# Reordering loads, transposes and attention steps in the first two blocks of a fused linear-attention and gated feed-forward kernel

## The chip, the cores and the metric

The kernel runs on one core of a Trainium2 chip. The metric is the device time of one execution in microseconds (us). The core's engines are TensorE (PE, with its weight loads as PEld), VectorE (DVE), ScalarE (ACT), GpSimd (POOL) and SyncE (SP); each takes its own instructions in the order in which the program lists them and waits on semaphores for the others. DMAs issued by POOL go to one software queue, those issued by SP to one hardware queue; both are served by the core's 16 DMA engines.

## What is computed

```
kv  = einsum('bhsd,bhse->bhde', k, v)        # 8 batches, 8 heads, 576 tokens, head size 64
out = einsum('bhsd,bhde->bhse', q, kv)
x   = out / sqrt(mean(out*out, -1) + 1e-6) * g_norm      # then tokens x 512
g, val = x @ w_gate, x @ w_val               # 512 -> 1536
ffn = (gelu(g) * val) @ w_out                # 1536 -> 512
y   = x + sigmoid(x @ w_res) * ffn           # 4608 tokens x 512, float32
```

Inputs and outputs are float32. The kernel computes in float16 with float32 accumulation; the loads by POOL convert on the way.

## The kernel before, in words

**Blocks.** Tokens come in nine blocks. Block b (0 to 7) holds the first 512 tokens of batch b, as `NJ` = 4 tiles of 128; block 8 holds the 64 tokens that are left over of each batch. Attention for a batch is computed one or two blocks ahead of the block's feed-forward part, and its steps are put between the feed-forward matmuls so that PE always has work. The order on every engine is written out by hand: nothing is scheduled afterwards.

**Steps of attention for batch b.** `load_batch` (L117) issues on POOL the DMAs of q (into `qraw`), k, v, the last 64 rows of k and v (`load_last_kv`, L107: tiles `kl`, `vl`, two sets used in turn) and, for batches from 4 on, two `qr` pieces of leftover q rows. `by_token` (L128) reorders q; `a_qT` on PE (batch 1) or `d_qT` (L376, a DMA transpose on SP) makes `qT`. `a_kv` (L219) multiplies k by v into `kv2`, 40 small matmuls and a copy. `a_o` (L224) multiplies `qT` by `kv2` into four PSUM tiles (`op`). `a_ss` (L263) squares them on ACT and sums on DVE; `a_norm` (L298) turns the sums into `1/rms` with Newton steps on DVE or POOL; `a_t` (L337) scales on DVE into `t`. `a_xT` (L350, PE and ACT, batch 1) or `d_xT` (L387, a DMA transpose on SP) makes `xT`; `a_g` (L366) multiplies by g afterwards on DVE.

**Feed-forward.** In block 0 up to f = 7 and in block 1, `m_gval` (L421) computes a 128-wide slice f of gate and value for all 512 tokens, `m_act` applies gelu on ACT and multiplies on DVE into `hid`. Later slices and blocks use `gv_group` (L920), a seven-product scheme for 2 x 2 quarters, whose sums of weights (`weight_sums`, `wo_sums`, `wr_sums`) are made on DVE in blocks 0 and 1. Its words such as "1g" or "h22" name products and evacuations; "h22" is the last of a group and runs on POOL (L986). Functions hung on a word run right behind it. The output product is `out_by_f` (L1004) in block 0: twelve steps f, each of four matmuls (one per token tile) into four PSUM banks; later blocks use `out_by_products` (L608), with PSUM tiles wA, wD, wE, wF.

**What sets the order around the change.** Each block has a list of slots, one per slice f or output step, and a dictionary `plan` from slot to functions that run behind it. `attn_plan_1` (L1324) puts batch 1's attention into block 0's output slots: slot `NF + 3` (NF = 12) is the last of the four res products, slot `NF + 4 + f` is output step f. `plan_attn_2` (L1369) puts batch 2's into block 1 (slot s = slice s), `plan_attn_ahead` (L1399) batch 3's into block 1 and the later ones two blocks ahead. The steps below the `for blk` loop (L1527) emit it all; behind slot 2 of block 0 it loads w_res, batch 1 and w_out.

**Queues.** POOL's DMAs use eight semaphores in turn, so an issue waits until the DMA eight before it has landed; what POOL has to do behind it waits too. `load_behind(b)` (L1354) first lets POOL copy one element of `qT` of batch b into a tile `hold`, which makes POOL wait for that transpose, and then issues the loads of batch b + 1. SP holds the DMA transposes and the stores of results, strictly in the order of the program.

Before, the order of POOL's loads in block 0 is w_res, q, k, v, kl, vl of batch 1, then w_out in pieces of 2, 2, 4 and 4 slices. SP's order in block 1 is: qT of batch 2, four stores, qT of batch 3, xT of block 2, xT of block 3. PE's order at the end of block 1 is: kv of batch 3, eight res products (`rps`), op of batch 3, eight res products, wA.

Of the kernel before, what the change touches and what calls it, by code (L numbers as in the profile page):

```python
# [14 lines left out]
RMS_EPS = 1e-6  # L15
# [3 lines left out]
def kernel(  # L19
# [94 lines left out]
        b16_t[b, "k"] = qkvp.tile(by_head, FP16, tag="k16", name="k16")  # L114
        b16_t[b, "v"] = qkvp.tile([P, H, NJ * D], FP16, tag="v16", name="v16")

    def load_batch(b):  # L117
        tiles_16(b)
        raw[b, "q"] = stage.tile([P, H, NJ * D], FP16, tag="qraw", name="qraw")
        nc.gpsimd.dma_start(out=raw[b, "q"], in_=rows4(q, b, 0, H))  # L120
        nc.gpsimd.dma_start(out=b16_t[b, "k"], in_=rows4(k, b, 0, H))
        nc.gpsimd.dma_start(out=b16_t[b, "v"], in_=rows4(v, b, 0, H))
        load_last_kv(b)
        if pair(b) is not None:
            load_qr(2 * pair(b))
            load_qr(2 * pair(b) + 1)

    def by_token(b, copy=nc.vector.tensor_copy, js=slice(0, NJ)):  # L128
        copy(
# [168 lines left out]
    def a_norm(b, j0, j1, eng=nc.vector):  # L298

        s = st[b]  # L300
        if "rinv" not in s:
            s["rinv"] = attnp.tile([P, NJ + 1, H], FP32, tag="ny", name="ny")
        ss, yy = (t[:, j0:j1, :].rearrange("p j h -> p (j h)") for t in (s["ss"], s["rinv"]))
        n = (j1 - j0) * H
        m = attnp.tile([P, (NJ + 1) * H], FP32, tag="nm", name="nm")[:, 0:n]
        a = attnp.tile([P, (NJ + 1) * H], FP32, tag="na", name="na")[:, 0:n]
        mh = attnp.tile([P, (NJ + 1) * H], FP32, tag="nh", name="nh")[:, 0:n]
        magic = 0x5F1FFFF9 if eng is nc.gpsimd else 0x5F3759DF
        eng.tensor_scalar(out=m, in0=ss, scalar1=1.0 / D, scalar2=RMS_EPS, op0=ALU.mult, op1=ALU.add)
# [3 lines left out]
        if eng is nc.gpsimd:  # L313
            for step in range(2):
                eng.tensor_tensor(out=a, in0=yy, in1=yy, op=ALU.mult)
                eng.tensor_tensor(out=a, in0=a, in1=m, op=ALU.mult)
                c = (-0.703952253, 0.703952253 * 2.38924456) if step == 0 else (0.375, -1.25)
                eng.tensor_scalar(out=mh, in0=a, scalar1=c[0], scalar2=c[1], op0=ALU.mult, op1=ALU.add)
# [3 lines left out]
                eng.tensor_tensor(out=yy, in0=mh, in1=yy, op=ALU.mult)  # L322
            return
        eng.tensor_scalar(out=mh, in0=m, scalar1=-0.5, scalar2=None, op0=ALU.mult)
        for _ in range(3):
            eng.tensor_tensor(out=a, in0=yy, in1=yy, op=ALU.mult)
            eng.tensor_tensor(out=a, in0=a, in1=mh, op=ALU.mult)
            eng.scalar_tensor_tensor(out=yy, in0=a, scalar=1.5, in1=yy, op0=ALU.add, op1=ALU.mult)

    def pair(b):  # L330

        return b - B // 2 if b >= B // 2 else None
# [14 lines left out]
            scale = rinv[:, NJ, :, None].to_broadcast([P, H, D])  # L347
        nc.vector.tensor_tensor(out=t, in0=o, in1=scale, op=ALU.mult)  # L348

    def a_xT(b, j):  # L350
# [5 lines left out]
        nc.scalar.activation(  # L356
            out=xT_t[blk][:, jj, :, :], in_=ps, func=AF.Copy, scale=gcol
        )

    def a_x(b, j, eng=nc.vector):  # L360
        row_times_g(*where(b, j), eng)
# [56 lines left out]
                stop=(cc == NP - 1 and j1 == NJ),  # L418
            )

    def m_gval(blk, f, pool=pmoe, tag="mm"):  # L421
        if f == 0:
            hids[blk] = hidp.tile([P, NF, NJ * P], FP16, tag="hid", name="hid")
        gps = pool.tile([P, NJ * P], FP32, tag=tag, name="gps")
        m_mm(gps, wg_c, f, blk, 0, NJ)
        vps = pool.tile([P, NJ * P], FP32, tag=tag, name="vps")
        m_mm(vps, wv_c, f, blk, 0, NJ)
        m_act(blk, f, gps, vps)

    def m_res(blk, j, bank):  # L430
# [489 lines left out]
    def gv_group(blk, g, banks, amid, order):  # L920
# [67 lines left out]
        for word in ORDERS[order].split():  # L988
# [12 lines left out]
            for f in amid.get(word, ()):  # L1001
                f()

    def out_by_f(blk):  # L1004

        ths, fpss, pfs, banks = [], [], [], {}

        def res(j):
            if j == 0:
                banks.update(banks_behind())  # L1010
            ths.append(m_res(blk, j, banks[j]))

        slots = [lambda j=j: res(j) for j in range(NJ)]

        def step(f):
            if f == 0:
                fpss.extend(pmoe.tile([P, C], FP32, name="fps", bank=banks[n]) for n in "ADEF")
                pmoe.turn = [banks[n] for n in "ADEF"]
            for j in range(NJ):
                m_ffn(blk, j, f, fpss[j])  # L1020
            if NFH <= f < NFH + NJ:
# [302 lines left out]
    def attn_plan_1():  # L1324

        b = 1
        ss = [lambda j=j: a_ss(b, j) for j in range(NJ)]
        t = [lambda j=j: a_t(b, j) for j in range(NJ)]
        x = [lambda j=j: a_xT(b, j) for j in range(NJ)]
        plan = {  # L1330
            NF - 1: [lambda: by_token(b)],
            NF + 3: [
                lambda: attn_begin(b),
                lambda: a_qT(b, 0),
                lambda: a_qT(b, 1),
                lambda: load_batch(b + 1),
                lambda: a_kv(b),
                *[lambda j=j: a_x(0, j) for j in range(NJ)],
            ],
            NF + 4: [lambda: a_o(b), ss[0], ss[1]],  # L1340
            NF + 5: [ss[2], ss[3]],
            NF + 6: [lambda: a_norm(b, 0, NJ), t[0], t[1], t[2], t[3]],
            2 * NF: [x[0], x[1]],
            2 * NF + 1: [x[2]],
            2 * NF + 2: [x[3], lambda: wo_sums(0), lambda: wo_sums(2)],
        }
        return plan

    plans = [{} for _ in range(B + 1)]
# [19 lines left out]
    def plan_attn_2():  # L1369
        b, m = 2, 1  # L1370
        act = nc.scalar.copy
        at(m - 1, 2 * NF + 3, lambda: by_token(b, act, slice(0, 2)))
        at(m, 0, lambda: by_token(b, act, slice(2, 4)), lambda: attn_begin(b), lambda: d_qT(b))
        at(m, 2, lambda: a_kv(b))
        at(m, 3, lambda: load_behind(b))
        at(m, 1, lambda: wo_sums(1))
        at(m, 3, lambda: wo_sums(3))
        at(m, 4, lambda: a_o(b))
        for j in range(NJ):
            at(m, 4 + j // 2, lambda j=j: a_ss(b, j))  # L1380
        at(m, 6, lambda: a_norm(b, 0, NJ, nc.gpsimd))
        for j in range(NJ):
            at(m, 9 + j // 2, lambda j=j: a_t(b, j))
        at(m, 10, lambda: d_xT(b, 0, NJ))
        for i in range(2):
            amid_out.setdefault(m, {}).setdefault("00", []).insert(i, lambda i=i: a_g(b, 2 * i, 2 * i + 2))

# [11 lines left out]
    def plan_attn_ahead(b):  # L1399
# [22 lines left out]
        else:  # L1422
            at(m, 8, lambda: by_token(b, act, slice(0, 2)))
            at(m, 9, lambda: by_token(b, act, slice(2, 4)), *begin)
            at(m, NF - 1, lambda: a_kv(b, act))
            at(m, NF, lambda: load_behind(b))
        if rem:
            at_word(m + 2, 0, "cv", lambda: a_g(b, NJ, NJ + 1))
            own = 2 * pair(b) + 1 == b
# [3 lines left out]
                at_word(m, last, "3g", lambda: rem_mm(b))  # L1433
            at_word(m, last, "g12", lambda: rem_out(b))
        else:
            at(m, NF, lambda: a_o(b), lambda: a_ss(b, 0), lambda: a_ss(b, 1))
            aside_out(m, "D", lambda: a_ss(b, 2), lambda: a_ss(b, 3))
        aside_out(m, "F", lambda: a_norm(b, 0, NJ + rem, pool))
        first = [lambda: new_block(b), lambda: a_t(b, 0), lambda: a_t(b, 1)]
# [23 lines left out]

    units = [(n, g) for g in (1, 2, 0) for n in "gv"]
    sums = {u: weight_sums(u, nc.vector) for u in units}
    for slot, u in ((2, ("g", 1)), (4, ("g", 2)), (NF - 1, ("v", 1))):
        for i in range(2):
            at(0, slot + i, *sums[u][2 * i : 2 * i + 2])
    at(0, 6, *sums["v", 2][0:2])
    at_word(0, 0, "1v", *sums["v", 2][2:4])  # L1470
    late_sums = [f for u in (("g", 0), ("v", 0)) for f in sums[u]]
    for i, f in enumerate(late_sums[0:6]):
        at(1, (2, 6, 7)[i // 2], f)
    aside_out(1, "D", *late_sums[6:8])
    for blk in GROUPS:
        t = token_sums(blk, nc.vector)
# [50 lines left out]
    for blk in range(B + 1):  # L1527
# [21 lines left out]
        else:  # L1549
# [25 lines left out]

                plan.setdefault(NF - 2, []).append(banks_ahead)
            if blk == 1:
                slots[0] = lambda: m_gval(1, 0, pattn, "at")
            outs = []
            slots += [lambda i=i: outs[i]() for i in range(4 if blk < B else 2)]  # L1580
            if not groups:
                plan.setdefault(NFH + 2, []).insert(0, lambda: s_begin(blk))

            def products(blk=blk, outs=outs):
                if not res_in_halves(blk) and not res_and_attn(blk):
# [18 lines left out]
        for s in range(len(slots)):  # L1604
# [42 lines left out]
```

## Time and profile before

| what | value |
|---|---|
| median of three runs | 321.18 us (320.92 to 321.63) |
| span of the profiled execution, first to last instruction | 319.6 us |
| difference to the median, taken as what lies around the span | 1.6 us |
| PE / DVE / ACT / POOL busy | 309.5 / 275.2 / 210.8 / 188.0 us |
| granted TensorE clock over the span | 0.999 |
| PE's idle time that a wait for vl ended, at 42 us | 0.28 us |
| PE's idle time that a wait for w_out ended, at 43 us | 0.63 us |
| block 0's output products, first and last | 43.53, 54.61 us |
| block 1's slices (`m_gval`), first to the end of the last | 55.55 to about 77.8 us |
| op of batch 3 / first output product of block 1 | 80.49 / 82.80 us |
| first product of block 2 | 91.97 us |

The profile lists instruction groups with engine, source line, output and input tiles. A bracket behind a row of the timeline gives how long the engine had been idle before it, and whose event ended that. Matmuls overlap in time: their pace is read from start to start (0.216 us for 512 columns, 0.109 for 256), not from the duration of one.

### The profile page before, as it was taken

To read this page: it belongs to the slowest core of one execution; us is meant where nothing else is said; L and a number is where in the kernel's file an instruction comes from. 1 tells how busy PE (TensorE), PEld (TensorE's weight loads), DVE (VectorE), ACT (ScalarE), POOL (GpSimd) and SP (SyncE) were. 2 spreads that over 40 slices of the span, in tenths; PEclk is the share of its full clock that TensorE was granted. 3 is DMA by queue.
4 is the path that set the end of the run, shared out by engine and by line. 5 is a ranking of instruction groups with operands and counts; after the bars stand their busy time and mean duration, and the time that the engine had idled before them with its cause. 6 is when DMAs were issued, how large, how long until landed. Compare 5 with 4: busy or idle time off the path is not lost.

```text
span 319.6 us, 7753 instructions
## 1 busy us (share of the span) xinstructions
PE 309.5 (97%) x3039; PEld 245.6 (77%) x3039; DVE 275.2 (86%) x488; ACT 210.8 (66%) x385; POOL 188.0 (59%) x248
## 2 busy tenths in 40 slices
PE   7899989999999999999999999999999999999993
PEld 2544755444788888888888888888888888888882
DVE  5886979799898999989998999899988777897774
ACT  4763675456848794879587858795767467736770
POOL 2873350573769479756875887517761375396332
PEclk9999999999999999999999999999999999999999
DMA  7999999799994699479947694800340003000204
GB/s 253 328 192 202 195 203 196 162 153 189 171 118 82 199 138 97 82 216 128 105 84 215 88 145 71 226 6 0 68 148 2 0 3 132 2 2 40 93 0 131
DMA packets 77253, 38.89 MB, mean 122 GB/s; under 512 B 42146, under 2 KB 74914, under 8 KB 77218
## 3 DMA queue, kind: packets, MB, share of 16 engines
q0 software_dynamic: 39280, 17.17, 42.7%
q1 hardware_dynamic: 37360, 20.71, 24.8%
q10 hardware_dynamic: 578, 0.52, 0.5%
q8 instruction: 23, 0.38, 0.5%
q14 instruction: 12, 0.10, 0.1%
HBM read 38.80 MB, written 9.44 MB: 151 GB/s over the span
## 4 chain that ended last, share of the span: by engine, by line
PE 84%; DMA 11%; SPq 1%; POOL 1%; DVE 1%; issue 0%; DVEq 0%
PE Ag L949 12%; PE Av L949 11%; PE wA L518 11%; PE Fv L949 6%; PE Fg L949 6%; DMA wg<-in_moe_w_gate_dram 5%; DMA wo<-in_moe_w_out_dram 5%; PE rA L569 4%; PE gps L413 3%; PE fps L450 3%; PE vps L413 3%; PE Ev L949 3%; PE Eg L949 3%; PE wD L518 3%; PE wF L518 3%; PE wE L518 3%
## 5 line engine op out<-in xcount | busy, mean ns | idle before, releaser
L986 POOL TENSOR_TENSOR hid<-ge,c 128x512 f16<-128x512 f16 x22 | 25.6, 1164 | 37.9 <-ACT ge L980 37.9
L518 PEld LDWEIGHTS <-hid_s 128*128 128x128 f16 x384 | 37.6, 98 | 4.4
L949 PEld LDWEIGHTS <-wsv 128*128 128x128 f16 x352 | 34.1, 98 | 5.2 <-issue 1.1
L949 PEld LDWEIGHTS <-wsg 128*128 128x128 f16 x352 | 34.4, 98 | 4.0
L364 POOL TENSOR_TENSOR t<-t,g 128x512 f16<-128x512 f16 x32 | 37.1, 1188 | 0.0
L705 POOL TENSOR_TENSOR osb<-osb,t 128x512 f32<-128x512 f32 x28 | 34.1, 1246 | 0.0
L959 ACT COPY Eg<-Ag 128x512 f32<-128x512 f32 x22 | 12.8, 584 | 27.9 <-PE Ag L949 27.9
L518 PEld LDWEIGHTS <-hid 128*128 128x128 f16 x288 | 28.2, 98 | 3.5
L949 PEld LDWEIGHTS <-wg 128*128 128x128 f16 x264 | 25.8, 98 | 3.2
L949 PEld LDWEIGHTS <-wv 128*128 128x128 f16 x264 | 25.8, 98 | 3.0
L949 PE MATMUL Av<-ts,wsv 128*128 128x256 f16 x176 | 26.4, 272 | 0.1
L949 PE MATMUL Ag<-ts,wsg 128*128 128x256 f16 x176 | 26.4, 273 | 0.0
L970 DVE TENSOR_TENSOR Fg<-Ag,d 128x512 f32<-128x512 f32 x22 | 15.3, 697 | 11.0 <-ACT d L963 8.1
L261 DVE TENSOR_REDUCE ss<-sq 128x8 f32<-128x512 f32 x32 | 20.5, 679 | 2.4 <-ACT sq L256 2.4
L401 ACT ACTIVATE ge<-gps 128x512 f16<-128x512 f32 x20 | 11.9, 598 | 15.6 <-PE gps L413 13.6
L518 PE MATMUL wA<-wo_ts,hid_s 128*128 128x256 f16 x168 | 20.6, 273 | 0.0
L980 ACT ACTIVATE ge<-Eg 128x512 f16<-128x512 f32 x22 | 13.2, 598 | 9.9 <-PE Eg L949 9.9
L980 ACT ACTIVATE ge<-c 128x512 f16<-128x512 f32 x22 | 13.8, 627 | 7.7 <-DVE c L970 7.7
L413 PE MATMUL vps<-xT,wv 128*128 128x512 f16 x72 | 18.5, 379 | 0.4 <-DMA wv<-in_moe_w_val_dram 0.3
L348 DVE TENSOR_TENSOR t<-op,ny 128x512 f16<-128x512 f32 x28 | 18.4, 684 | 0.5 <-POOL ny L322 0.4
L970 DVE TENSOR_TENSOR c<-Ag,d 128x512 f32<-128x512 f32 x22 | 15.2, 689 | 3.9 <-PE Ag L949 3.8
L413 PE MATMUL gps<-xT,wg 128*128 128x512 f16 x72 | 18.5, 379 | 0.0
(220 smaller groups left out, 851.0 us busy)
## 6 DMA issues: line engine op xcount, KB each, us to landing
out_dram<-osb SPq DMA_DIRECT2D x14, 512.0 KB, 3.4
qraw<-in_q_dram POOLq DMA_DIRECT2D x7, 512.0 KB, 6.5
k<-in_k_dram POOLq DMA_DIRECT2D x7, 512.0 KB, 8.4
v<-in_v_dram POOLq DMA_DIRECT2D x7, 512.0 KB, 10.4
wg<-in_moe_w_gate_dram POOLq DMA_DIRECT2D x2, 512.0 KB, 9.5
wo<-in_moe_w_out_dram POOLq DMA_DIRECT2D x2, 512.0 KB, 13.6
out_dram<-osb SPq DMA_DIRECT2D x4, 256.0 KB, 3.8
wv<-in_moe_w_val_dram POOLq DMA_DIRECT2D x3, 256.0 KB, 8.5
```

What stands on the lines that cost most here:

```text
L261: nc.vector.tensor_reduce(out=out_, in_=sqs.pop((b, i)), op=ALU.add, axis=mybir.AxisListType.X)
L348: nc.vector.tensor_tensor(out=t, in0=o, in1=scale, op=ALU.mult)
L364: eng.tensor_tensor(out=t_t[blk][:, jj, :], in0=t_t[blk][:, jj, :], in1=g16, op=ALU.mult)
L413: nc.tensor.matmul(ps[:, j0 * P : j1 * P], lhsT=w[:, cc, :], rhs=xT_t[blk][:, j0:j1, cc, :], start=(cc == 0 and j0 == 0), stop=(cc == NP - ...
L518: nc.tensor.matmul(ps[:, e - es[0], :], lhsT=a[:, f, e * P : (e + 1) * P], rhs=b[:, f, :], start=(start and e == es[0] and f == 0), stop=( ...
L569: nc.tensor.matmul(out_[:, e, :], lhsT=x_[:, e, cc, :], rhs=w_[:, cc, :], start=(first and e == 0 and cc == 0), stop=(cc == 1), skip_group ...
L705: nc.gpsimd.tensor_tensor(out=res_all[of], in0=res_all[of], in1=t_t[blk][of], op=ALU.add)
L949: nc.tensor.matmul(out_[:, r, :], lhsT=lhsT, rhs=rhs, start=(first and r == 0 and c == 0), stop=(c == 1), skip_group_check=True,)
L959: nc.scalar.copy(out=tile_of("E", u), in_=ps["A", u])
L970: nc.vector.tensor_tensor(out=dst, in0=ps["A", u], in1=sb["d", u], op=ALU.add)
L980: nc.scalar.activation(out=ge[q], in_=source(q, "g"), func=AF.Gelu)
L986: eng.tensor_tensor(out=dst, in0=ge[q], in1=source(q, "v"), op=ALU.mult)
```

## The change

- **Loads in block 0.** `load_batch` calls `amid()` between k and v; for batch 1 that loads w_out's first three slices. The rest of w_out follows in pieces of 1, 2, 3 and 3. For all batches the two `qr` pieces go ahead of k.
- **Batch 1's attention** goes amid the output products of block 0. `a_kv` runs behind output step 2 with its copy on ACT; `a_o` and the squares behind the second matmul of step 3; norm and `t` behind step 4; the four `a_xT` behind step 10, amid step 11 (two, the second with its copy on DVE) and at its end. `out_by_f` gets hooks between its matmuls for that (`amid_step`). Block 1's first slice is multiplied in two halves of tokens.
- **`a_norm` on DVE** has nine instructions instead of twelve: the two steps that POOL used, with constants folded.
- **`wo_sums`**: all four in block 1 (slots 1, 1, 3, 4); before, two of them stood in block 0 and two in slots 1 and 3. `s_begin` in blocks without groups goes from slot 8 to slot 10; two late weight sums go from slots 6, 7 to 9, 10.
- **Batch 2**: op behind slot 5 instead of 4, norm on DVE behind slot 7 instead of on POOL behind slot 6, `t` in slots 8 and 9 instead of 9 and 10, `d_xT` behind slot 9 instead of 10. By that xT of block 2 stands ahead of qT of batch 3 in SP's order.
- **Batch 3**: kv behind the first eight res products, op behind all sixteen.
- **Batch 4's loads** wait on POOL for qT of batch 3 and also for xT of block 2; its kl and vl leave `load_batch` and are issued in block 2, behind the POOL product of group 1 ("h22").

```diff
-    def load_batch(b):
+    def load_batch(b, amid=lambda: None):
         nc.gpsimd.dma_start(out=raw[b, "q"], in_=rows4(q, b, 0, H))
-        nc.gpsimd.dma_start(out=b16_t[b, "k"], in_=rows4(k, b, 0, H))
-        nc.gpsimd.dma_start(out=b16_t[b, "v"], in_=rows4(v, b, 0, H))
-        load_last_kv(b)
         if pair(b) is not None:
             load_qr(2 * pair(b))
             load_qr(2 * pair(b) + 1)
+        nc.gpsimd.dma_start(out=b16_t[b, "k"], in_=rows4(k, b, 0, H))
+        amid()
+        nc.gpsimd.dma_start(out=b16_t[b, "v"], in_=rows4(v, b, 0, H))
+        if pair(b) != 0:
+            load_last_kv(b)
...
-        eng.tensor_scalar(out=mh, in0=m, scalar1=-0.5, scalar2=None, op0=ALU.mult)
-        for _ in range(3):
-            eng.tensor_tensor(out=a, in0=yy, in1=yy, op=ALU.mult)
-            eng.tensor_tensor(out=a, in0=a, in1=mh, op=ALU.mult)
-            eng.scalar_tensor_tensor(out=yy, in0=a, scalar=1.5, in1=yy, op0=ALU.add, op1=ALU.mult)
+        eng.tensor_tensor(out=a, in0=yy, in1=yy, op=ALU.mult)
+        eng.tensor_tensor(out=a, in0=a, in1=m, op=ALU.mult)
+        eng.scalar_tensor_tensor(out=mh, in0=a, scalar=2.38924456, in1=yy, op0=ALU.subtract, op1=ALU.mult)
+        eng.tensor_tensor(out=a, in0=mh, in1=mh, op=ALU.mult)
+        eng.tensor_tensor(out=a, in0=a, in1=m, op=ALU.mult)
+        eng.scalar_tensor_tensor(
+            out=yy, in0=a, scalar=1.25 / (0.375 * c**2), in1=a, op0=ALU.subtract, op1=ALU.mult
+        )
+        eng.scalar_tensor_tensor(
+            out=yy, in0=yy, scalar=1.875 / (0.375 * c**4), in1=mh, op0=ALU.add, op1=ALU.mult
+        )
...
         gps = pool.tile([P, NJ * P], FP32, tag=tag, name="gps")
-        m_mm(gps, wg_c, f, blk, 0, NJ)
         vps = pool.tile([P, NJ * P], FP32, tag=tag, name="vps")
-        m_mm(vps, wv_c, f, blk, 0, NJ)
+        for j in range(0, NJ, step):
+            m_mm(gps, wg_c, f, blk, j, j + step)
+            m_mm(vps, wv_c, f, blk, j, j + step)
...
                 lambda: load_batch(b + 1),
-                lambda: a_kv(b),
                 *[lambda j=j: a_x(0, j) for j in range(NJ)],
             ],
-            NF + 4: [lambda: a_o(b), ss[0], ss[1]],
-            NF + 5: [ss[2], ss[3]],
-            NF + 6: [lambda: a_norm(b, 0, NJ), t[0], t[1], t[2], t[3]],
-            2 * NF: [x[0], x[1]],
-            2 * NF + 1: [x[2]],
-            2 * NF + 2: [x[3], lambda: wo_sums(0), lambda: wo_sums(2)],
+            NF + 6: [lambda: a_kv(b, nc.scalar.copy)],
+            NF + 8: [lambda: a_norm(b, 0, NJ), *t],
+            2 * NF + 2: [x[0]],
         }
+        amid_step[3, 1] = [lambda: a_o(b), *ss]
+        amid_step[NF - 1, 1] = [x[1], lambda: a_xT(b, 2, nc.vector)]
+        amid_step[NF - 1, 3] = [x[3]]
...
-        at(m, 1, lambda: wo_sums(1))
-        at(m, 3, lambda: wo_sums(3))
-        at(m, 4, lambda: a_o(b))
+        at(m, 1, lambda: wo_sums(0), lambda: wo_sums(1))
+        at(m, 3, lambda: wo_sums(2))
+        at(m, 4, lambda: wo_sums(3))
+        at(m, 5, lambda: a_o(b))
         for j in range(NJ):
-            at(m, 4 + j // 2, lambda j=j: a_ss(b, j))
-        at(m, 6, lambda: a_norm(b, 0, NJ, nc.gpsimd))
+            at(m, 5 + j // 2, lambda j=j: a_ss(b, j))
+        at(m, 7, lambda: a_norm(b, 0, NJ))
         for j in range(NJ):
-            at(m, 9 + j // 2, lambda j=j: a_t(b, j))
-        at(m, 10, lambda: d_xT(b, 0, NJ))
+            at(m, 8 + j // 2, lambda j=j: a_t(b, j))
+        at(m, 9, lambda: d_xT(b, 0, NJ))
...
-            at(m, NF - 1, lambda: a_kv(b, act))
-            at(m, NF, lambda: load_behind(b))
+            at(m, NF, lambda: a_kv(b, act), lambda: load_behind(b, b - 1))
+            at_word(m + 1, 1, "h22", lambda: load_last_kv(b + 1))
...
-            at(m, NF, lambda: a_o(b), lambda: a_ss(b, 0), lambda: a_ss(b, 1))
+            at(m, NF + 1, lambda: a_o(b), lambda: a_ss(b, 0), lambda: a_ss(b, 1))
...
-        at(1, (2, 6, 7)[i // 2], f)
+        at(1, (2, 9, 10)[i // 2], f)
...
-                load_batch(1)
-                for f0, f1 in ((0, 2), (2, 4), (4, 8), (8, NF)):
+                load_batch(1, lambda: load_wo(0, 3))
+                for f0, f1 in ((3, 4), (4, 6), (6, 9), (9, NF)):
                     load_wo(f0, f1)
```

More of the change, by code (lines that the diff above doesn't have):

```diff
@@ L307, in a_norm @@
         mh = attnp.tile([P, (NJ + 1) * H], FP32, tag="nh", name="nh")[:, 0:n]
-        magic = 0x5F1FFFF9 if eng is nc.gpsimd else 0x5F3759DF
-        eng.tensor_scalar(out=m, in0=ss, scalar1=1.0 / D, scalar2=RMS_EPS, op0=ALU.mult, op1=ALU.add)
+        pool = eng is nc.gpsimd
+        c = 0.703952253
+        scaled = 1.0 if pool else (0.375 * c**5) ** -2
+        magic = 0x5F1FFFF9 if pool else 0x5F1FFFF9 - 2**31
+        eng.tensor_scalar(
+            out=m, in0=ss, scalar1=scaled / D, scalar2=scaled * RMS_EPS, op0=ALU.mult, op1=ALU.add
+        )
         eng.tensor_scalar(
@@ L312, in a_norm @@
         )
-        if eng is nc.gpsimd:
+        if pool:
             for step in range(2):
@@ L316, in a_norm @@
                 eng.tensor_tensor(out=a, in0=a, in1=m, op=ALU.mult)
-                c = (-0.703952253, 0.703952253 * 2.38924456) if step == 0 else (0.375, -1.25)
-                eng.tensor_scalar(out=mh, in0=a, scalar1=c[0], scalar2=c[1], op0=ALU.mult, op1=ALU.add)
+                of_a = (-c, c * 2.38924456) if step == 0 else (0.375, -1.25)
+                eng.tensor_scalar(out=mh, in0=a, scalar1=of_a[0], scalar2=of_a[1], op0=ALU.mult, op1=ALU.add)
                 if step == 1:
@@ L323, in a_norm @@
             return
-        eng.tensor_scalar(out=mh, in0=m, scalar1=-0.5, scalar2=None, op0=ALU.mult)
-        for _ in range(3):
-            eng.tensor_tensor(out=a, in0=yy, in1=yy, op=ALU.mult)
-            eng.tensor_tensor(out=a, in0=a, in1=mh, op=ALU.mult)
-            eng.scalar_tensor_tensor(out=yy, in0=a, scalar=1.5, in1=yy, op0=ALU.add, op1=ALU.mult)
+        eng.tensor_tensor(out=a, in0=yy, in1=yy, op=ALU.mult)
[8 more added lines that the diff above has]
+            out=yy, in0=yy, scalar=1.875 / (0.375 * c**4), in1=mh, op0=ALU.add, op1=ALU.mult
+        )
     def pair(b):
@@ L348, in a_t, with a_xT @@
         nc.vector.tensor_tensor(out=t, in0=o, in1=scale, op=ALU.mult)
-    def a_xT(b, j):
+    def a_xT(b, j, eng=nc.scalar):
         blk, jj = where(b, j)
@@ L355, in a_xT @@
             nc.tensor.transpose(ps[:, cc, :], t_t[blk][:, jj, cc * P : (cc + 1) * P], ident)
-        nc.scalar.activation(
-            out=xT_t[blk][:, jj, :, :], in_=ps, func=AF.Copy, scale=gcol
-        )
+        if eng is nc.scalar:
+            nc.scalar.activation(out=xT_t[blk][:, jj, :, :], in_=ps, func=AF.Copy, scale=gcol)
+        else:
+            eng.tensor_scalar(out=xT_t[blk][:, jj, :, :], in0=ps, scalar1=gcol, scalar2=None, op0=ALU.mult)
     def a_x(b, j, eng=nc.vector):
@@ L419, in m_mm, with m_gval @@
             )
-    def m_gval(blk, f, pool=pmoe, tag="mm"):
+    def m_gval(blk, f, pool=pmoe, tag="mm", step=NJ):
         if f == 0:
@@ L1002, in gv_group @@
                 f()
+    amid_step = {}
     def out_by_f(blk):
@@ L1020, in step @@
                 m_ffn(blk, j, f, fpss[j])
+                for g in amid_step.get((f, j), ()):
+                    g()
             if NFH <= f < NFH + NJ:
@@ L1465 @@
     sums = {u: weight_sums(u, nc.vector) for u in units}
-    for slot, u in ((2, ("g", 1)), (4, ("g", 2)), (NF - 1, ("v", 1))):
+    for slot, u in ((2, ("g", 1)), (5, ("g", 2)), (NF - 1, ("v", 1))):
         for i in range(2):
             at(0, slot + i, *sums[u][2 * i : 2 * i + 2])
-    at(0, 6, *sums["v", 2][0:2])
+    at(0, 7, *sums["v", 2][0:2])
     at_word(0, 0, "1v", *sums["v", 2][2:4])
@@ L1577 @@
             if blk == 1:
-                slots[0] = lambda: m_gval(1, 0, pattn, "at")
+                slots[0] = lambda: m_gval(1, 0, pattn, "at", NJ // 2)
             outs = []
@@ L1581 @@
             if not groups:
-                plan.setdefault(NFH + 2, []).insert(0, lambda: s_begin(blk))
+                plan.setdefault(NF - 2, []).insert(0, lambda: s_begin(blk))
             def products(blk=blk, outs=outs):
```

## The prediction

> **What bounds the kernel now.** First the page: busy shares, then the chain that ended last.
>
> ```profile
> PE 309.5 (97%) x3039; PEld 245.6 (77%) x3039; DVE 275.2 (86%) x488; ACT 210.8 (66%) x385; POOL 188.0 (59%) x248
> ...
> PE 84%; DMA 11%; SPq 1%; POOL 1%; DVE 1%; issue 0%; DVEq 0%
> ```
>
> PE (TensorE) is the bound: whatever makes PE wait lengthens the kernel one for one, and only an idle stretch of PE can be won. Work elsewhere costs nothing unless PE waits for it. So I read PE's timeline from 37 us on (earlier the two kernels are alike) for gaps.
>
> ```profile
> 41.62 0.32 PE L211 MATMUL kvp<-v,k 128*64 128x64 f16 x8
> 42.21 0.22 PE L211 MATMUL kvp<-vl,kl 128*64 128x64 f16 x2 [0.28 <-DMA vl<-in_v_dram]
> ...
> 43.53 1.04 PE L450 MATMUL fps<-wo,hid 128*128 128x512 f16 x4 [0.63 <-DMA wo<-in_moe_w_out_dram]
> 44.50 0.64 PE L233 MATMUL op<-kv,qT 64*128 64x64 f16 x32
> ```
>
> The bracket is the idle time before a row and what ended it. Batch 1's kv takes 43.53 - 41.62 = 1.91 us up to the first output product; undisturbed (batch 2's) it takes 0.76, from 60.82 to 61.58. So 1.15 us are lost, and this is all that the change can win: from there to 116 us PE's rows follow each other without a bracket of this size.
>
> **Part by part, step by step.**
>
> *Loads of w_out and v.* The software queue runs one after the other: landings (issue plus time to landing) are k 38.7, v 41.3, kl and vl 41.8 and 42.2, w_out slices 43.5, 44.8, 47.2, 49.8. That is 2.6 us for v, 0.42 for kl or vl, 2.5 for four slices, so 0.63 a slice. In the new order: three slices at 40.6, v 43.2, vl 44.1, the fourth slice 44.7. Twelve products (0.216 us each: 32 of them take 45.08 to 51.99) fill 41.55 to 44.15; kv then finds vl, products of slice 3 follow at 45.0 and find it landed. Margins are about 0.25 us. POOL's hid product (L986, 37.03) now stands behind a DMA issue that waits for k's landing, so it ends near 40.9; its reader is product step 9, after 49 us. The next batch's loads queue behind a full ring, so their later issue costs nothing.
>
> *kv to output products.* The kv copy moves to ACT; kv's start to the copy's end took 1.23 us for batch 3 (77.90 to 79.13). Only two products stand between, so op starts at about 45.5 (44.50 before). Behind it, before: 11.05 us to block 1's first product at 55.55, with 44 output products; now ten fewer: 45.5 + 11.05 - 2.16 = 54.4, plus 0.1 for one more switch and 0.1 for t's fourth tile. I take 54.6: **a gain of 0.9 us**. The shorter DVE norm (nine instructions for twelve, 0.22 us apart) is what lets t keep up. DVE's xT copy and block 1's first product in halves cost nothing while the other half streams (0.87 us); uncovered, about 0.4.
>
> *DVE in block 1.* DVE now holds all four wo_sums and batch 2's norm. From the second hid (58.65; before 59.27, the gelu ahead of it now waits for ACT's q copies) to the end of batch 2's t: nine hid at 0.61, four wo_sums at 0.91, eight weight sums 1.7, kv copy 0.4, reductions 2.4, norm nine at 0.225 = 2.0, t 2.4: 18.1 us, plus 0.8 idle for squares and products, ends at **77.5**. It cannot end before 76.4: t follows the hid of f = 9, whose products end at 73.5, then hid, sums and t are 2.7. The hids themselves come in time for PE's banks.
>
> *SyncE's order.* This is what decides. SP's timeline, then rates of two stretches (the last two columns are the DMA share and GB/s):
>
> ```profile
> 75.25 1.71 SPq L377 DMA_TRANSPOSE qT<-q  x1
> 78.33 21.82 SPq L390 DMA_TRANSPOSE xT<-t  x2
> ```
>
> ```profile
> 76.50:79.00 2.50, 2.50 (x49) 1.41 (x48) 2.46 (x6) 0.84 (x2) 0.00 (x0) 1.00 1.08 207
> 99.50:102.50 3.00, 3.00 (x30) 2.68 (x29) 1.99 (x4) 2.56 (x5) 3.00 (x4) 1.00 1.10 211
> ```
>
> Batch 3's qT is issued at 75.25 and lands 4.3 us later; batch 2's xT is issued behind it. In the new program xT stands first, and SP waits there for batch 2's t. So xT issues at 77.5, and qT behind it: one transpose is 512 KB, 2.53 us at 207 GB/s; the second row holds two transposes back to back at 211, so the rate is one for both. qT lands at 77.5 + 4.3 + 2.5 = **84.3**.
>
> PE's turn for batch 3's op, before and now:
>
> ```profile
> 80.49 0.64 PE L233 MATMUL op<-kv,qT 64*128 64x64 f16 x32
> 81.06 1.90 PE L433 MATMUL rps<-wr,xT 128*128 128x512 f16 x8
> 82.80 1.47 PE L518 MATMUL wA<-wo,hid 128*128 128x256 f16 x12
> ```
>
> Block 1 takes 22.3 us from its first product to its last (55.55 to 77.81), then the first eight rps 1.73, kv 0.85, the other eight 1.73: 54.6 + 26.6 = 81.2. **PE waits 3.1 us for qT.** Behind the wait stand op and all output products; wA starts at 84.3 + 0.67 = 85.0 instead of 82.8. The trace holds no such pair with both ends wanted, so bounds: if two transposes ran together at the 397 GB/s that stores reach at 107 to 109 us, qT lands at 82.0 (wait 0.8); if the pair ran like the disturbed xT of 78.33, which took 6.0, qT lands at 77.5 + 1.9 + 6.0 = 85.4 (wait 4.2). I take 84.3, from the back-to-back row.
>
> [...]
>
> *Behind the wait.* op is now directly ahead of wA, so squares, reductions and norm come later relative to PE. Before:
>
> ```profile
> 85.47 1.28 DVE L261 TENSOR_REDUCE ss<-sq 128x8 f32<-128x512 f32 x2 [0.47 <-ACT sq L256]
> 87.00 0.70 DVE L481 TENSOR_TENSOR wF<-wA,wd 128x512 f32<-128x512 f32 x1 [0.25 <-PE wA L518]
> ...
> 91.22 0.69 DVE L348 TENSOR_TENSOR t<-op,ny 128x512 f16<-128x512 f32 x1 [0.38 <-POOL ny L322]
> ...
> 93.01 0.69 DVE L348 TENSOR_TENSOR t<-op,ny 128x512 f16<-128x512 f32 x1
> ```
>
> DVE now runs two reductions 85.4 to 86.6, hid_s 0.9, weight sums 1.2, reductions to 90.0, wF to 90.65; PE wants bank A again at 85.0 + 4 x 1.31 = 90.2: 0.45 us. POOL's norm takes 4.35 (86.84 to 91.18), so t begins at 94.4; its second tile frees a bank at 96.9 where block 2 asks for it at 96.5: another 0.45. Before, that margin was 0.2 (93.70 against 93.88). Bounds for each: 0 to 0.8. POOL issues batch 4's loads from 84.5 to 89.3, so they end just ahead of its norm; if not, t is later by as much.
>
> *Batch 4's kl and vl* move behind the POOL product that runs at 105.19 to 106.35, and are wanted at 109.52 (before's times):
>
> ```profile
> 105.19 1.16 POOL L986 TENSOR_TENSOR hid<-ge,c 128x512 f16<-128x512 f16 x1 [0.48 <-ACT ge L980]
> ...
> 109.52 0.20 PE L211 MATMUL kvp<-vl,kl 128*64 128x64 f16 x2
> ```
>
> The nearest row of a load on an empty queue is the q issued at 111.71: first bytes 1.7 us later, some 128 KB by 3.5, landing signal about 0.4 more: 106.4 + 3.9 = 110.3, a wait of 0.8. Bounds: 0 (in a running stream the two take 0.84), and 1.8 if the stores that fill all queues at 107 to 109 share with it. Batches 5 to 7 load kl and vl 0.9 us later, 18 us ahead of need: nothing.
>
> *Sum* on PE: -0.9 + 3.1 + 0.45 + 0.45 + 0.8 = +3.9. The profiled execution's span is 319.6; the median of three runs, 321.18, has 1.6 around it. 319.6 + 3.9 + 1.6 = 325.1; I say **325.0**.
>
> Does PE's idling also cost clock? The first five 512-wide products take 1.18 to 3.42, about 0.43 us each, against 0.216 later: PE starts at half pace. [...] From the rows alone: 9 such products at the start lose 0.21 each, 1.9 in all; that is the upper end, and I take nothing.
>
> **The rivals.**
> 1. *The wait exists but is short* (0.8 to 2): DVE or the queue is quicker than I add up. For it: 76.4 is DVE's earliest end, and t alone moves the landing one for one. The stalls behind shrink with it. -0.9 + 1.7 + 0.5 = +1.3: 322.5. Chance 0.16.
> 2. *Faster*: one mechanism, batch 3's qT lands before PE's op at 81.2. It decides if xT could be issued by 81.2 - 6.8 = 74.4. Then only the 0.9 is left and kl and vl hide: 320.3. Against it: f = 9's products end at 73.5 and three DVE groups follow. Chance 0.04.
> 3. *The change does not do what it says in block 0*: v or vl lands late and kv waits as before. The gain is gone, but op's time is set by DVE and SP, which shift by less: about 325.3, within the likeliest case.
> 4. *The idle PE loses its clock*, or kl and vl take their upper end: +5.5 to +6, 327. Chance 0.07.
> 5. *Even*: wait near 1, all else hidden: 321.2. Chance 0.03.
>
> The likeliest case, 324 to 326.5, has 0.70. Range 322.3 to 327.2: from rival 1 to the upper bounds of the wait (4.2) and of the stalls behind. A difference under 0.2% cannot be told from no change here. Faster 0.04, same 0.03, slower 0.93.
>
> **What would show it.** In the changed profile: no bracket for vl or w_out at 41 to 46; block 1 beginning near 54.6; a bracket of about 3 us at batch 3's op, released by the DMA of qT; small brackets at the third wA and at block 2's first Fv; one for vl before batch 4's kv. I am wrong if op of batch 3 has no bracket, or if SP issues qT ahead of xT.

## The result, and the profile after

The changed kernel takes **330.44 us** (median of six runs, 328.36 to 331.78); the kernel before, run beside it, 321.17 (320.69 to 321.63). The ratio is 1.029, with a 95% interval of 1.027 to 1.031: 9.3 us slower, where 3.8 were forecast, and above the range's end of 327.2. The direction was right, the size was not.

The profiled execution took 330.3 us, with a span of 328.5 against 319.6: 8.9 us more. The page already tells where to look. In the row of the granted clock, over 40 slices of 8.2 us, two slices stand out; before, every slice was 9.

```profile
PEclk9999999999799979999999999999999999999999
```

The 7s are the slices from 82 and from 115 us. In the timeline of PE these are the places, first around batch 3's op:

```profile
84.70 0.64 PE L235 MATMUL op<-kv,qT 64*128 64x64 f16 x32 [3.80 <-DMA qT<-q]
85.28 1.96 PE L535 MATMUL wA<-wo,hid 128*128 128x256 f16 x12
87.04 2.70 PE L535 MATMUL wD<-wo_ts,hid_s 128*128 128x256 f16 x12
89.57 1.47 PE L535 MATMUL wA<-wo_ts,hid_s 128*128 128x256 f16 x12
```

The wait for qT is the one forecast: 3.80 us against 3.1. But read the starts behind it: from wD to the next wA are 2.53 us for twelve 256-wide matmuls. Before, wA began at 82.80, 85.42 and 88.04, with one such group between each two: 1.31 us a group.

```profile
85.42 1.47 PE L518 MATMUL wA<-wo_ts,hid_s 128*128 128x256 f16 x12
```

In the changed kernel PE runs at half pace until 89.5. Then the second place, batch 4's kv:

```profile
113.50 0.32 PE L213 MATMUL kvp<-v,k 128*64 128x64 f16 x8
116.60 0.22 PE L213 MATMUL kvp<-vl,kl 128*64 128x64 f16 x2 [2.79 <-DMA vl<-in_v_dram]
...
117.46 1.03 PE L966 MATMUL Fv<-xT,wsv 128*128 128x256 f16 x4
118.29 1.06 PE L966 MATMUL Ag<-ts,wg 128*128 128x256 f16 x4
119.14 1.06 PE L966 MATMUL Av<-ts,wv 128*128 128x256 f16 x4
```

Again a wait, 2.79 us for vl instead of 0.8, and again half pace behind it: four matmuls take 0.85 us from start to start, in the undisturbed block 0.44. The queue of SP shows the swap of the two transposes as forecast; xT is issued at 76.85 (forecast 77.5) and qT, behind it, lands at 84.66 (forecast 84.3).

```profile
76.85 1.75 SPq L406 DMA_TRANSPOSE xT<-t  x1
78.77 3.80 SPq L393 DMA_TRANSPOSE qT<-q  x1
```

In block 0 the wait for w_out is gone, one of 0.49 us for vl is left, and block 1 begins at 54.09 instead of 55.55.

```profile
43.84 0.22 PE L213 MATMUL kvp<-vl,kl 128*64 128x64 f16 x2 [0.49 <-DMA vl<-in_v_dram]
...
54.09 0.60 PE L429 MATMUL gps<-xT,wg 128*128 128x256 f16 x4
```

Not all of these 1.46 us are the change's. From 8.5 to 19.4 us PE's rows in the two traces lie within 0.03 us of each other. Then, still ahead of the changed steps, the kernel before falls behind by 1.18 us. More than half of that, 0.62 us, arises at slices whose weights, asked for at the same time in both (from 15.1 us on), landed 0.63 us later in its profile (the first at 23.05 against 22.42). Three of the later profiles with the new order, in which these weights landed at 22.74 to 23.61, lose 0.4 to 0.8 us in the same place, so this comes from the execution and not from the change. The whole queue was late by the same 0.63 (batch 1's k landed at 38.69 against 38.06), and before the change the output products waited for its w_out; so, as an estimate, 0.63 of the 1.46 are the execution's and 0.83 the change's.

Comparing the same instruction in both traces gives the whole account. How much later (or earlier) than before it starts:

| PE's row | before | after | later by | this stretch adds |
|---|---|---|---|---|
| first rps of block 0 | 37.18 | 36.00 | -1.18 | -1.18 ahead of the changed steps |
| first product of block 1 | 55.55 | 54.09 | -1.46 | -0.28 block 0 |
| first wA | 82.80 | 85.28 | 2.48 | +3.94 wait for qT 3.80, rest 0.14 |
| second wA | 85.42 | 89.57 | 4.15 | +1.67 half pace |
| first Ag of block 2 | 91.97 | 96.12 | 4.15 | 0 |
| fourth rA of block 2 | 116.06 | 124.74 | 8.68 | +4.53 wait for vl 2.79, half pace and rest 1.74 |
| end | 319.63 | 328.51 | 8.88 | +0.20 |

### The profile page after: what moved, and what is told of

It is laid out like the page before. It is cut to its first block, busy times and chain, and to the rows that moved or that the text cites. A ratio compares the mean times of both kernels' runs of the same rounds, so it can differ in the third digit from the quotient of the medians.

```text
span 328.5 us, 7766 instructions
## 1 busy us (share of the span) xinstructions
PE 313.8 (96%) x3047; PEld 248.9 (76%) x3047; DVE 277.6 (85%) x494; ACT 210.3 (64%) x385; POOL 183.9 (56%) x238
## 4 chain that ended last, share of the span: by engine, by line
PE 78%; DMA 14%; DVE 3%; POOL 2%; SPq 1%; issue 1%; ACT 1%; DVEq 0%
PE wA L535 11%; PE Ag L966 11%; PE Av L966 11%; DMA vl<-in_v_dram 6%; PE Fv L966 6%; PE Fg L966 5%; DMA wg<-in_moe_w_gate_dram 5%; PE rA L586 4%; PE gps L429 3%; PE vps L429 3%; PE wD L535 3%; PE wF L535 3%; PE wE L535 3%; PE Eg L966 3%; PE Ev L966 3%; PE w L535 2%
## 5 line engine op out<-in xcount | busy, mean ns | idle before, releaser
L1003 DVE TENSOR_TENSOR hid<-ge,Fv 128x512 f16<-128x512 f16 x22 | 15.0, 682 | 5.3 <-ACT o L296 4.2
L429 PE MATMUL gps<-xT,wg 128*128 128x512 f16 (+1 forms) x76 | 18.7, 368 | 0.0
L429 PE MATMUL vps<-xT,wv 128*128 128x512 f16 (+1 forms) x76 | 18.7, 368 | 0.0
```

The source lines that it names most:

```text
L429: nc.tensor.matmul(ps[:, j0 * P : j1 * P], lhsT=w[:, cc, :], rhs=xT_t[blk][:, j0:j1, cc, :], start=(cc == 0 and j0 == 0), stop=(cc == NP - ...
L1003: eng.tensor_tensor(out=dst, in0=ge[q], in1=source(q, "v"), op=ALU.mult)
```

## The experiments

Theory A: two waits of PE, each with a stretch of half pace that follows from the idling. Its rivals stand with each run. The expectations call the runs by labels (e1 to e13); these stand in brackets behind the headings. Each time is a median beside the kernel before on the same chip (321.4 us for the first four kernels, 320.8, 321.6 and 321.3 for the later groups).

### Batch 4's kl and vl back (e1)

```diff
-        if pair(b) != 0:
-            load_last_kv(b)
+        load_last_kv(b)
...
-            at_word(m + 1, 1, "h22", lambda: load_last_kv(b + 1))
```

> Batch 4's kl and vl are issued by its load_batch again, in block 1, instead of behind block 2's h22; the rest is as in the changed kernel. Theory A (two separate waits of PE, each with its own stretch of half pace behind it): the vl wait of 2.79 us and the 1.5 us of half pace behind it go, op's wait for qT of batch 3 stays at 3.8: 330.4 - 4.4 = about 326.0. Rival B (one cause: the swap on SP makes everything behind it late, the loads too): the wait at batch 4's kv changes its name to v or k, the time falls by under 1.5: 329 or more.

Measured: 326.25 us (325.96 to 328.26). The wait for vl and the half pace behind it are gone, the op of batch 3 is as it was:

```profile
84.15 1.03 PE L234 MATMUL op<-kv,qT 64*128 64x64 f16 x32 [3.81 <-DMA qT<-q]
85.11 2.74 PE L534 MATMUL wA<-wo,hid 128*128 128x256 f16 x12
```

4.2 us for this part, as theory A had it; rival B falls.

### The order on SP back (e2)

```diff
-        at(m, 9, lambda: d_xT(b, 0, NJ))
+        at(m, 10, lambda: d_xT(b, 0, NJ))
```

> Only the order on SP is undone: xT of block 2 is issued behind slot 10, so behind qT of batch 3. Theory A: op's wait of 3.8 us and the 1.67 of half pace behind it go, the wait for vl stays at about 2.8 with its 1.5: 330.4 - 5.5 = about 325, up to 326 if the stalls at wF and at block 2's Fv that the prediction named now come out. Rival B (the vl wait is a consequence of the late block 1): vl's wait goes too, 320 to 321.

Measured: 327.73 us (326.13 to 328.46), 2.7 less and not 5.5. The wait for qT is gone and the one for vl stays (2.37 us), so rival B falls here too. The half pace behind vl is there as before. But waits of 0.37 for wF, 0.55 for t and 0.65 for the copy Eg have come in, in which PE loses 2.1 us, counted from start to start. They are the stalls that the prediction had named behind the wait, and they are larger than the 0.9 it gave them.

### Both back (e3)

> Both undone: xT behind qT on SP, and kl and vl of batch 4 in load_batch. Theory A: only block 0's gain is left (block 1 began 1.46 us earlier in the changed kernel's profile) against 0.2 later: 319.9, faster than before by about 1.3. Rival D (the gain of block 0 is an accident of one execution, and the steps that moved to DVE take it back): 321.2 or more.

Measured: 324.66 us (322.97 to 325.75). Theory A's 319.9 fails, and the number alone is one that rival D allows. But block 1 begins at 54.21 in this profile, so what block 0 gave is still there, and a third loss comes behind it, 3.4 us from start to start. PE's timeline of this kernel:

```profile
87.32 1.47 PE L534 MATMUL wA<-wo_ts,hid_s 128*128 128x256 f16 x12 [0.37 <-DVE wF L497]
...
90.34 1.47 PE L534 MATMUL wA<-wo_ts,hid 128*128 128x256 f16 x12 [0.24 <-DVE osb L497]
...
94.15 0.60 PE L965 MATMUL Fg<-ts,wsg 128*128 128x256 f16 x4 [1.47 <-DVE t L362]
95.40 0.60 PE L965 MATMUL Ag<-ts,wsg 128*128 128x256 f16 x4 [0.65 <-ACT Eg L975]
```

The largest names t, which waits on DVE for POOL's norm of batch 3. So POOL's timeline:

```profile
83.24 0.18 POOL L1377 COPY hold<-xT 1x1 f16<-1x1 f16 x1 [3.63 <-DMA xT<-t]
83.78 0.93 POOL L120 DMA_DIRECT2D qraw<-in_q_dram  x1 [0.36 <-ACT wE L706]
...
89.28 0.48 POOL L313 TENSOR_SCALAR nm<-ss 128x32 f32<-128x32 f32 x1
```

POOL waits 3.63 us for xT of block 2 before it issues batch 4's loads, and the norm stands behind these issues (L313 begins at 89.28; before the change 86.84). The sums it needs were there at 86.6.

### The hold on xT out as well (e4)

```diff
-            at(m, NF, lambda: a_kv(b, act), lambda: load_behind(b, b - 1))
+            at(m, NF, lambda: a_kv(b, act), lambda: load_behind(b))
```

> As e3_both, and the loads of batch 4 wait on POOL for qT of batch 3 only, as before the change, not for xT of block 2 too. In e3's profile POOL starts these eight issues at 83.8 instead of 80.1 and its norm of batch 3 at 89.3 instead of 86.8, and PE waits 1.5 us for t (and 0.65 for the copy Eg behind it) in block 2. Theory E (the hold on xT keeps POOL's norm back): the norm starts near 87, the waits at block 2's Fg shrink from 2.1 to under 0.5: 324.7 - 2 = about 322.5; the waits of 0.4 and 0.25 at the third wA and behind it stay. Rival F (DVE's extra work alone makes t late): no change from 324.7.

Measured: 321.68 us (321.37 to 322.74), ratio 1.001 (0.999 to 1.004): 3.0 less than with the hold (2.4 if each is taken against its own runs of the kernel before, and 2.4 between the spans of the two profiles), and not to be told from the kernel before. POOL's rows answer to those above:

```profile
80.05 0.93 POOL L120 DMA_DIRECT2D qraw<-in_q_dram  x1 [0.71 <-ACT kv L223]
...
86.64 0.21 POOL L313 TENSOR_SCALAR nm<-ss 128x32 f32<-128x32 f32 x1 [1.17 <-DVE ss L262]
```

The norm now waits for its sums and not for POOL, so theory E holds. The waits for wF (0.37) and Eg (0.41) stay and cost PE 1.1 us from start to start, about what block 0 had given. Three edits hold 8.8 of the 9.3 us.

### The hold alone out (e13)

The same line, in the changed kernel with the rest of it as it was.

> The changed kernel with POOL's wait for xT of block 2 ahead of batch 4's loads taken out, and nothing else; the wait for qT of batch 3 stays. Theory E, with the hold hidden: in the changed kernel xT lands at 82.9 and qT at 84.7, so POOL starts the loads at qT's landing with or without the hold: 330.4, no difference. Rival J (the hold costs its 3 us here too, as between e3 and e4): 327.5.

Measured: 330.06 us (329.34 to 330.22), within the changed kernel's runs. So the hold's 2.4 to 3.0 us are hidden in the changed kernel, since qT lands after xT (84.7 and 82.9 us in the changed kernel's profile) and POOL waits for both; the order on SP had covered another loss. This is part of why undoing the swap alone gave 2.7 us: in that kernel's profile POOL waits 3.67 us for xT and t comes late. The rest, the wait for wF among it, was not taken apart.

### PE kept busy during the wait for qT (e5)

```diff
+            if b == 3 and jj == 0:
+                for _ in range(14):
+                    nc.tensor.matmul(
+                        o[0].rearrange("p j r d -> p (j r d)"),
+                        lhsT=xT_t[1][:, 0, 0, :], rhs=wr16[:, 0, :], start=True, stop=True,
+                    )
```

> The changed kernel with 14 extra 512-wide matmuls of w_res ahead of batch 3's op, into the PSUM bank that op then overwrites: 3.0 us of work inside the 3.8 us wait. Theory A with the clock as the price of idling: op's wait shows as under 1 us, the half pace from 86.4 to 89.6 is gone, the granted clock is higher and the time falls by 1.6 to about 328.8. Rival C (the half pace has another cause, such as the transposes or the late start of wA): half pace stays, 330.4.

Measured: 327.59 us (326.97 to 328.27): 2.9 less, with 14 matmuls more. PE's timeline:

```profile
80.32 3.18 PE L234 MATMUL op<-wr,xT 128*128 128x512 f16 x14
84.29 0.64 PE L241 MATMUL op<-kv,qT 64*128 64x64 f16 x32 [0.79 <-DMA qT<-q]
84.86 1.48 PE L541 MATMUL wA<-wo,hid 128*128 128x256 f16 x12
86.18 1.47 PE L541 MATMUL wD<-wo_ts,hid_s 128*128 128x256 f16 x12
```

op starts when it did (qT still decides), and behind it every twelve matmuls take 1.32 us. The half pace comes from the idling; rival C falls. In this execution there was no half pace behind the vl wait either (2.44 us), so more went than the 1.6 expected. In return small waits of 0.22 us for wF and 0.41 for Eg came in, which cost PE 1.0 us from start to start: with its pace whole, PE reaches these tiles before DVE and ACT are done.

### Fewer matmuls in that wait, and both waits filled (e12, e8)

Four instead of 14 matmuls ahead of op; and, in another kernel, the 14 and 24 of 256 columns ahead of batch 4's kv.

> The changed kernel with 4 extra 512-wide matmuls (0.87 us) ahead of batch 3's op, so that about 2.9 us of its wait of 3.8 are left idle. If an idle time between 2.5 us (no half pace behind it in the profiles of e2 and e5) and 3.8 us (half pace in all) is what matters: half pace in some executions, a time between e5's 327.6 and the changed kernel's 330.4. If any idle time of over 2.5 us costs it: 330.4.

Measured: 329.81 us (329.06 to 330.75), nearer to the second case, in which the price stays. In the profile 3.06 us were left idle, and half pace followed.

> As e5_fill_op, and 24 extra 256-wide matmuls (2.6 us) ahead of batch 4's kv, into the PSUM tile that kv then overwrites. Theory A: the clock stays whole in every run; the wait for vl remains as time, but no half pace follows, so the runs lie close together near the lowest of e5's, 327.0, and the spread of the runs (3.4 us in the changed kernel) falls below 1 us. Rival C (the spread has another cause): the same median and spread as e5.

Measured: 328.24 us (327.41 to 328.84), no better than one wait filled, and the spread of 1.4 us stayed: this expectation failed. The profile has no half pace in it; but its block 0 waited 0.84 us for w_out, and block 1 began at 55.14 instead of 53.66. Between the 13 profiles of this order the start of block 1 differs by 2.4 us (53.43 to 55.84); whether this is what spreads these four runs was not tested. Their granted clocks are 0.995 to 1.000, and the times do not follow them. In the changed kernel's six runs they do: 328.36 us at 0.995, 329.25 to 330.58 at 0.986 to 0.990, 331.58 and 331.78 at 0.981. There the lost clock goes with the spread.

The profiles of the runs give a list of PE's idle times after 36 us and of what followed. Half pace (10 to 22 matmuls of 256 columns at 0.21 us instead of 0.109) behind 2.37, 2.48, 2.79, 3.06, 3.12, 3.75, 3.80, 3.81 and 3.81 us; none behind 1.42, 1.47 and 2.44. (The expectation of the four-matmul run is wrong on one point: behind the 2.37 us of the kernel with the order on SP back there was half pace.) The length alone does not decide: 2.37 us brought it and 2.44 did not.

The granted clock in the traces shows what does. It steps between 1.00 and 0.50, and within a profile its changes lie whole multiples of 3.41 us apart: 86.13, 89.54, 116.85 and 120.26 in the changed kernel. So a trace can be cut into stretches of 3.41 us on these marks. In the rows, the length is followed by PE's busy time (with its instructions), the granted clock, the DMA share and GB/s. The changed kernel:

```profile
82.72:86.13 3.41, 1.43 (x40) 1.00 0.51 117
86.13:89.54 3.41, 3.41 (x18) 0.50 0.74 74
113.44:116.85 3.41, 0.62 (x39) 1.00 0.89 154
116.85:120.26 3.41, 3.41 (x43) 0.50 0.94 109
```

And the run with 14 matmuls, whose 2.44 us without half pace fall across a mark:

```profile
110.97:114.39 3.42, 1.81 (x37) 1.00 1.15 220
114.39:117.80 3.41, 2.57 (x50) 1.00 0.38 35
```

In all nine cases PE had been idle for 1.99 to 2.89 us of the stretch that ends where the half pace begins. In every other stretch at the full clock ahead of the last product it was idle for 1.90 us or less, and the clock stayed. Half pace then lasted one stretch, or two (e1 and e6) where 1.2 us or more of the wait still lay in the first. Where the limit lies between 1.90 and 1.99, and whether it matters what PE does in the rest of the stretch, no run tried.

### Without the stores beside kl and vl (e6)

```diff
+                if blk != 1:
+                    at_word(blk + 1, 1, "h22", lambda i=i: store(i))
```

> The changed kernel without the two stores of block 1's 512 rows (1 MB; these rows of the output are left unwritten), which SP issues at 109.0 to 110.6, beside kl and vl. Theory A (kl and vl share the DMA engines with these stores): vl lands 3.9 us behind its issue at most, as the prediction took for an idle queue, so at 115.1 or sooner, and PE's wait at batch 4's kv falls from 2.8 to 1.3 or less, with no half pace behind it: 330.4 - 3 = about 327.5. Rival G (the software queue is that slow by itself for these small rows): vl's landing and the wait stay within 0.4 us: 330.

Measured: 326.85 us (325.01 to 327.57). The wait and the time of the two loads:

```profile
114.95 0.22 PE L213 MATMUL kvp<-vl,kl 128*64 128x64 f16 x2 [0.52 <-DMA vl<-in_v_dram]
```

```profile
kl<-in_k_dram POOLq DMA_DIRECT2D x1, 64.0 KB, 3.4
vl<-in_v_dram POOLq DMA_DIRECT2D x1, 64.0 KB, 3.1
```

In the changed kernel these two rows (KB each, median us from issue to landing) say 4.9 and 5.4. From kl's issue to vl's landing are 3.88 us here, just the 3.9 that the prediction took, and 6.15 beside the stores, which moved 1 MB from 109.0 to 115.0. Theory A holds, and the 2.3 us that the stores cost are what the prediction missed.

### Batch 3's order back, block 0 alone, sums later (e9, e11, e10)

The remaining runs ask what block 0's gain is worth. In the first, kv and op of batch 3 also go back to their slots.

> As e4_no_hold, and the kv and op of batch 3 go back to their slots of before (kv ahead of the res products, op amid them), so that from batch 2's t on only the DVE work is moved. Theory E: the waits for wF and osb go too, nothing of the changed kernel's losses is left and block 0's gain of about 1.3 us stands: 320.0, faster than before. Rival F (DVE carries too much in block 1): a wait for wF or t of 0.5 to 1.5 us stays: 321 to 322.

Measured: 321.98 us (321.24 to 323.52), ratio 1.003 (1.000 to 1.005), 2 above the expectation. In its profile block 0 waits for both loads again, and qT of batch 3 took 6.7 us from issue to landing, where the same transpose in the same place took 4.3 before:

```profile
42.16 2.76 PE L466 MATMUL fps<-wo,hid 128*128 128x512 f16 x12 [0.46 <-DMA wo<-in_moe_w_out_dram]
...
82.35 0.64 PE L234 MATMUL op<-kv,qT 64*128 64x64 f16 x32 [1.42 <-DMA qT<-q]
```

These are mishaps of one execution, the slowest of the ten (323.52 us). They do not explain the median, and its cause stays open; nothing follows for the order itself.

> Block 0's edits alone (w_out and v, batch 1 amid the output products, slice 0 in halves, the norm of nine instructions for batch 1, all four wo_sums in block 1); batch 2, batch 3, batch 4's loads and the order on SP are as before the change. Theory H (the gain of block 0 is real, 1.0 to 1.5 us as in most profiles so far, and what ate it in e4 and e9 lies in the later blocks): 0.7 to 1.5 us below the kernel before. Rival I (the margins of 0.2 us in the new order of loads turn each slow DMA into a wait of PE, which takes the gain back): within 0.5 us of the kernel before, with waits for vl or w_out in the profile.

Measured: 320.55 us (320.02 to 323.65) beside 321.6, ratio 0.9995 (0.997 to 1.002). The medians differ by 1.05 us as theory H has it, the interval takes in no gain at all. Block 1 begins at 53.78 in its profile.

The sums moved in the last kernel:

```diff
-    aside_out(1, "D", *late_sums[6:8])
+    aside_out(1, "01", *late_sums[6:8])
...
-    aside_out(1, "D", wr_[3])
+    aside_out(1, "end", wr_[3])
```

> As e4_no_hold, with the last two sums of gate and value weights and the last one of w_res (1.2 us on DVE) behind the output product that frees block 1's second tile, instead of ahead of batch 3's last reductions. Theory E: these reductions, wF and POOL's norm come 1.2 us earlier, the waits of 0.53 for wF and 0.57 behind t go: 321.7 - 1.0 = 320.7, at or 0.5 below the kernel before. Rival F (DVE is full from 76 to 96 us, and what is moved back makes t or Fg late): 321.5 or more.

Measured: 321.30 us (lowest 320.14), ratio 0.9998 (0.997 to 1.002). wF's wait is gone, but the one for Eg grew from 0.41 to 0.66 us and one of 0.51 for t came in: two of the moved sums took 1.55 us together instead of 0.49 while POOL multiplied beside them, and t stood behind them. That the two engines got in each other's way is read from their times alone and was not tested. No version here is shown to beat the kernel before.

## Why the prediction was wrong

- **Block 0, "a gain of 0.9 us":** right in mechanism, and near in size as far as can be told. The profiles differ by 1.46, of which some 0.8 is the change's by the estimate above; the medians differ by 1.05 with block 0 alone, not secured by the interval. That 1.46 exceeds the 1.15 that the prediction called "all that the change can win" is due to the late loads in the profile before. The margins of 0.25 us were as thin as stated: in 11 of the 13 profiles with this order block 1 began between 53.4 and 54.2, in two at 55.1 and 55.8, each with a wait for w_out.
- **"PE waits 3.1 us for qT":** right, 3.80 measured, inside its bounds of 0.8 to 4.2. xT was issued 0.65 us earlier than forecast, the two transposes took 7.8 us from the first issue instead of 6.8, and PE came 0.3 earlier.
- **"Does PE's idling also cost clock? ... I take nothing":** this is the step that failed most. Idling cost 1.67 us behind op and 1.60 behind vl (from vl's matmul to the fourth rA, 8.14 us instead of 6.54), 3.3 of the 5.0 us by which the span went beyond the forecast. That a wait of 3.1 us would cost no clock was the author's estimate: no row of the trace gave a length below which idling is free of it, and no run shows a wait of that length that was. With both ends known (0 and 1.9) the low one was taken, once, although the forecast itself held a second wait. The runs showed in its place that some 2 us of idling inside one of the clock's stretches of 3.41 us were enough (1.99 behind op): waits of 3.06 and 3.12 us already brought half pace, and whether a shorter one did went by where it fell (2.37 did, 2.44 did not).
- **"a wait of 0.8" for kl and vl:** mechanism right, size wrong: 2.79. The 3.9 us for an idle queue were right to the tenth, and the stores that the prediction saw at 107 to 109 us were known to share; they cost 2.3, where the bound of 1.8 for the wait had left them 1.0.
- **wF and t, 0.45 each:** neither showed. With the order on SP back they came out as 2.1 us, and with kl and vl back too as 3.4 (from start to start). PE lost its clock just there, so DVE and POOL had caught up by the time it asked; with the pace kept by 14 extra matmuls, the waits for wF and Eg were there and cost 1.0 us. (The margin of 0.2 that the prediction read at t before the change was smaller: 93.88 is the chain's time for Fv, and in PE's timeline Fv starts at 93.75, 0.05 behind t's end.)
- **The hold on xT** was costed at nothing, with the remark that POOL's issues end just ahead of its norm. True in the changed kernel; its cover was the wait for qT, and its price without that cover 2.4 to 3.0 us, which the prediction did not give.
- **The rivals:** the fourth (lost clock, 327, chance 0.07) was the nearest, but it added one loss of clock or a longer vl wait, where both came, and the clock twice. The range ended at 327.2 because of that. The low end of its +5.5 to +6 has no row behind it; in the runs a restart measured 1.60 and 1.67 us, with which 3.9 becomes 5.5 to 5.6.

In sum, from the account above: -1.46 + 3.94 + 1.67 + 2.79 + 1.74 + 0.20 = 8.88 us. Against the forecast's 3.9 these are 4.98 more: block 0 -0.56, op's wait +0.84, half pace and rest +3.41, vl's wait +1.99, wF and t -0.90, the end +0.20.

## What to carry to other kernels

A wait that leaves PE idle for 2 us or more is to be costed with a restart at half pace on top, here 1.1 to 2.3 us each behind waits of 2.37 to 3.81 us (none behind one of 2.44), and two waits with two. Up to about 4 us, an estimate (twice the 1.99 us that were enough in one stretch of 3.41), it depends on where the wait falls in the stretches; by the same estimate a longer one leaves enough of itself in one of them wherever it falls. Two DMAs that are each in time alone need not be in time in one queue (qT behind xT landed 5.9 us after its issue instead of 4.3, and PE waited 3.80) or on the same DMA engines (vl beside the stores took 5.4 us instead of 3.1, and PE waited 2.79): list who is issued ahead on the queue and what else moves in the five microseconds before the data is wanted. And when a wait is taken away, ask what it covered: here 5.6 us stood in one wait and the half pace behind it, and its removal alone gave 2.7, with a hold on another engine showing in its place.

## What the runs showed of the hardware that was not expected

- Half pace after idle times from 2.37 us on, for 10 to 22 matmuls of 256 columns, and once none (2.44 us). The granted clock changes only on marks 3.41 us apart; it fell where PE had been idle for 1.99 us or more between two marks (nine cases) and never where it was 1.90 or less.
- A DMA transpose of 512 KB, batch 3's qT issued ahead of xT, took 4.3 us from issue to landing in the kernel before and 6.7 in the run with batch 3's order back, xT's transpose being issued 3.0 to 3.1 us behind it in both.
- The software queue's pace wavers: w_out's first three slices landed 1.9 us behind k in the changed kernel and 2.95 in the run with batch 3's order back; the last three 2.0 us behind the piece before them and 3.7 in the run with both waits filled.
- Two loads of 64 KB took 3.1 to 3.4 us by themselves and 4.9 to 5.4 beside 1 MB of stores.
